# One scale total per expert, a larger VectorE share for the S4 work, and a third block of the last expert but one that multiplies by seven twice

## The chip, the cores and the metric

The program runs on one core of a Trainium2 chip. The metric is the device time of one execution in microseconds (us); the kernel before takes 2319.49 us as the median of three runs (2318.05 to 2320.9). TensorE (PE in the profile) multiplies, VectorE (DVE), ScalarE (ACT) and GpSimd (POOL) work on the elements, SyncE (SP) and GpSimd issue most of the transfers. Each engine takes its instructions strictly in the order in which the program wrote them, so an instruction that waits holds up all that stands behind it on its engine.

## The reference

2048 tokens of 512 numbers are normalized (layernorm). Two branches run on the result and are added to the input:

```python
x = A_u
xn = _layernorm(x, axis=-1)
return x + _A_ref(xn, ...) + _B_ref(xn, B_w_gate, B_w1, B_w2)
# A (S4): a kernel K[d, l] = Re(sum over n of C * exp(dt*A*l) * dt*B), 128 modes n, and a causal
#         convolution of each of the 512 channels with it by FFT, plus u * Dskip
# B (MoE): eight experts, all eight chosen for each token (K = 8), with softmax gates:
for e in range(E):
    h = _silu(xf @ w1[e]) @ w2[e]      # 512 -> 1792 -> 512
    out = out + w * h
```

## The kernel before, in words

**Experts and blocks.** The experts e run from 0 to 7, and each takes the tokens in four blocks tb of 512; (e, tb) names a block here. A float32 operand is split into a high and a low half in f16, and a product is three matmuls (high by high, high by low, low by high). The first product (x by w1) of every block but (0, 0) goes by a seven-product scheme in the manner of Strassen. The second one (hidden values by w2) is plain in the function `block`: 168 matmuls with 512 columns for a block. In `block2` it goes by seven products as well: 294 matmuls with 256 columns, while the first product falls into 588 matmuls with 128 columns where `block` has 294 with 256. The set `strong` lists the blocks that take `block2`: the four of expert 7, and (6, 1) and (6, 2).

**Weights.** One buffer holds the split weights of one expert; the next expert's are made while the last block of the one before runs and in its own first block. `piece_w1` or `piece_w1x` makes w1's (a split on ScalarE, its low part on VectorE, sums on VectorE), `piece_w2` w2's, and `piece_w2x` the four sums of w2's quarters that only `block2` uses (four sums on VectorE, a split of 1024 elements on ScalarE at L493, its low part on VectorE at L496). The place of the w2 sums (`w2x`) lies where the S4 branch has its tiles, so that `open_second` makes it only when S4 is over. `plan(e)` writes the order of these pieces out by hand, and `work_on(limit)` takes up to so many steps of them at the end of each slot.

**Slots.** A block has four quarters d with four slots s each, 16 slots in all. In `slot` the program emits some matmuls of the second product, the pieces of the next weights, and a share of S4. `bg_run` keeps an account: it gives S4 `SHARE` (0.96) times the planned TensorE time of the slot, less what VectorE was given besides, and never carries more than one slot's credit over.

**Scales.** Before its weights are split, an expert's w1 and w2 are squared on ScalarE and summed (`piece_square`, `piece_end`, `prepass_end`). Each of the two takes a total over the partitions: a matmul of one column against ones in the shared PSUM bank "s4" (`pow2_total`), a copy on ScalarE, and a few VectorE operations of one column.

**S4.** 32 chunks of 16 channels: tables on VectorE (`s4_basis` for two chunks, `s4_tables`), the kernel's matmuls (kgen, L871), the transforms of kernel and input (kf, uf), the convolution in frequency space on VectorE (`s4_conv`, L989 to L1007), the way back (yp, L1028), and `s4_out`, which scales into the tile `ysb` on ScalarE (L1036) and sends it. All of these matmuls use the bank "s4" in turn. At the first strong block, `bg_until("s4")` writes out whatever is left of S4, without any expert's matmul between, before the block starts.

Of the kernel before, what the change touches and what calls it, by code (L numbers as in the profile page):

```python
# [9 lines left out]
F32 = mybir.dt.float32  # L10
# [3 lines left out]
AF = mybir.ActivationFunctionType  # L14
# [19 lines left out]
def s4_moe_kernel(  # L34
# [151 lines left out]
    def pow2_scale(dst, st, nm, add=0):  # L186

        it = sb.tile([P, st.shape[-1]], I32, tag="p2b", name=f"it_{nm}", bufs=2)
        V.tensor_scalar(it, st.bitcast(I32), 24, 23, op0=ALU.logical_shift_right, op1=ALU.logical_shift_left)
        V.tensor_scalar(dst.bitcast(I32), it, -1.0, float((204 + add) << 23), op0=ALU.mult, op1=ALU.add)  # L190

    def pow2_inverse(dst, src, add=0):

        V.tensor_scalar(dst.bitcast(I32), src.bitcast(I32), -1.0, float((254 + add) << 23), op0=ALU.mult, op1=ALU.add)
# [258 lines left out]
        times(sc[:, 3:4], sc[:, 0:1], 1 - ASH)  # L453

    def prepass_end(e, w, n):
        r = sb.tile([P, 1], F32, tag="r2", name=f"r2_{e}_{w}")
        V.tensor_reduce(r, rows[e, w][:, :n], axis=AX.X, op=ALU.add)
        yield
        st = pow2_total(r, 1, f"w{e}_{w}")
        yield  # L460
        if bank["out"]:
            take_bank()
        if w == 0:
            sc = scales[e] = sb.tile([P, 5], F32, tag="sc", name=f"sc{e}", bufs=3)
            w1_scales(sc, st, f"w{e}")
        else:
            sc = scales[e]
            pow2_scale(sc[:, 1:2], st, f"v{e}")
            pow2_inverse(sc[:, 4:5], sc[:, 1:2])
            V.scalar_tensor_tensor(sc[:, 4:5], sc[:, 4:5], float(2.0 ** (XSH - 1 + ASH)), sc[:, 2:3], op0=ALU.mult, op1=ALU.mult)  # L470
            ge_ = sb.tile([P, NT], F32, tag="gse", name=f"gse{e}", bufs=3)
            gates_e[e] = ge_
            if e > 1:
                V.tensor_scalar(ge_, gate[:, :, e], sc[:, 4:5], None, op0=ALU.mult)

    def load_raw(e, w, pr, why):

# [14 lines left out]
    def hilo(dst, raw, sc):  # L492
        S.activation(dst[:, 0], raw, AF.Copy, scale=sc)  # L493

        def low():
            V.scalar_tensor_tensor(dst[:, 1], raw, sc, dst[:, 0], op0=ALU.mult, op1=ALU.subtract)  # L496
            clock["dve"] += tt_(raw.free_size())
        return low
# [30 lines left out]

    done = set()  # L530
    work = []
    strong = {(E - 1, tb) for tb in range(NB)} | {(E - 2, 1), (E - 2, 2)}
    live = {"n": 0, "tw": False}

    def piece_square(e, w, pr, ready):
        return Item(lambda: load_raw(e, w, pr, "pp"), [lambda raw: square(e, w, pr, raw)], ready)
# [16 lines left out]
    def piece_w2x(e, pr, ready):  # L553

        def s0(raw):
            clock["dve"] += 1.4
            it.at = now()
            for o, x, y, op in ((0, 0, 1, ALU.subtract), (1, 3, 1, ALU.subtract), (3, 0, 3, ALU.add), (2, 3, 2, ALU.subtract)):
                V.tensor_tensor(raw[:, o, :], raw[:, x, :], raw[:, y, :], op=op)

        def s1(raw):
            return hilo(second_half["w2x"][pr].rearrange("p a o d -> p a (o d)"), raw.rearrange("p o d -> p (o d)"),
                        scales[e][:, 1:2])
        it = Item(lambda: load_raw(e, 1, pr, "raw"), [s0, s1], ready)
        it.made = (e, "w2x", pr)
        return it
# [30 lines left out]
    def piece_end(e, w, n, ready):  # L597

        st = {"g": prepass_end(e, w, n)}

        def step(k):
            st["at"] = now()
            next(st["g"], None)
            done.add((e, w, k))
            clock["dve"] += (0.2, 0.0, 0.9)[k]

        def can_go():
            if "at" not in st:
                return ready()
            return now() > st["at"] + 1 and bank_free() and now() + 1 not in turns  # L610
        it = Item(None, [lambda raw, k=k: step(k) for k in range(3)], can_go)
        it.e, it.w, it.sums = e, w, False
        return [it]

    def fetch():
# [13 lines left out]
    def can(it):  # L629

        if not it.ready():
            return False
        if len(it.steps) == it.n and it.load is not None and now() < it.at + 2 and "w2 scale" in done:
            return False
        if it.sums and len(it.steps) == it.n:
            return not live["tw"]
        if it.sums and len(it.steps) == 1:
            return now() > it.at + (it.made[0] > 1)
        return len(it.steps) == it.n or it.load is None or now() > it.at
# [113 lines left out]
    def s4_basis(g):  # L753
# [61 lines left out]
        for i, o, n in ((0, 160, 128), (160, 288, 64)):  # L815
# [3 lines left out]
            V.scalar_tensor_tensor(im[:, b], zr[:, a], 2.0, im[:, a], op0=ALU.mult, op1=ALU.mult)  # L819
            V.tensor_tensor(zr[:, b], f[:, :n], r[:, :n], op=ALU.subtract)  # L820
            yield 4 * tt_(n)
        V.tensor_scalar(zi[:, 0], im, -1.0, None, op0=ALU.mult)
        s4["basis", g] = (wv, zr, zi)
        yield 0.4

    def s4_tables(c):
        g, h = c // 2, c % 2
# [204 lines left out]
        clock["pe"] += 0.68  # L1032

    def s4_out(c):
        ysb = p4.tile([P, 2, NS, DC], F32, tag="ysb", name=f"ysb{c}", bufs=1)
        S.activation(ysb, s4["yp", c].rearrange("p r d i -> p r i d"), AF.Copy, scale=s4["ks", c][:, 1:2])  # L1036
        nc.sync.dma_start(ys4[:, c * DC:(c + 1) * DC].rearrange("(m k r) d -> k r m d", k=P, r=2), ysb)

# [15 lines left out]
    def now():  # L1054
        return clock["slot"]
# [306 lines left out]
    def plan(e):  # L1362

        def at(tb):
            return lambda: (e - 1, tb) in done
        early_ = (e, 1) in strong and e == E - 2
        if (e, 0) not in strong:
            for n, w in ((0, 0), (0, 1)) + ((1, 0), (1, 1)) * early_:
                ready = at((0, 1, 2, 2)[2 * n + w] if early_ else 1 + w)
                for pr in range(NPR):  # L1370
                    work.append(piece_square(e + n, w, pr, ready))
                work.extend(piece_end(e + n, w, NPR, ready))

        def made(what, d):
            return lambda: (e - 1, NB - 1, what, d) in done and (e, "py".index(what), 2) in done
        a = [piece_w1(e, pr, made("p", d)) for d, prs in enumerate(DQS) for pr in prs]
        b = [piece_w2(e, pr, made("y", d)) for d, prs in enumerate(DQS) for pr in prs]
        free = lambda pr: (e - 1, NB - 2) not in strong or (e - 1, "w2x", pr) in done
        x = [piece_w2x(e, pr, lambda pr=pr: "pool" in second_half and (e, 1, 2) in done and free(pr)) for pr in range(NPR)]
        if (e, 0) in strong:  # L1380
            a = [piece_w1x(e, pr, made("p", d)) for d, prs in enumerate(DQS) for pr in prs]
            work.extend((x[0], x[1], a[0], x[2], a[1], x[3], a[2], a[3], b[0], b[1], a[4], b[2], a[5], a[6], b[3], x[4], b[4], x[5], b[5],
                         x[6], b[6]))
        else:
            work.extend((a[0], a[1], a[2], b[0], a[3], b[1], a[4], b[2], a[5], b[3], a[6], b[4], b[5], b[6]))
            if (e, 1) in strong:
                work.extend(x)
# [3 lines left out]
        yield from s4_all()  # L1391

    bg = background()
    SHARE = 0.96

    def bg_run():

# [162 lines left out]
    def at(n, f, where=side):  # L1560
        where.setdefault((0, n // 16, n % 16 // 4, n % 4), []).append(f)
# [80 lines left out]
    def slot(e, tb, d, s, pops):  # L1642
        for f in mid.get((e, tb, d, s), ()):
            f()
        if e + tb == 0:
            work_lows()
        if (e, tb) in strong:
            pop2(pops)
        elif order2 and order2[0] < (e, tb):
            pop2(max(9, 4 * pops))  # L1650
        elif (e, tb - 1) in strong:
            pop2(4 * pops)
        else:
            pop(pops)
        flush()
        if e == 0:
            work_lows()
        room = act_room()
        if room > 1.0 and run_later():
            room -= 1.6  # L1660
        for f in side.get((e, tb, d, s), ()):
            f()
        work_lows()
        if e + tb == 0 or tb == NB - 1:
            work_on(2 if e + tb == 0 or room > 2 and (e or d < 3) else 1)
        elif e == 0 and tb == 1:
            work_on(2 if (d, s) < (2, 1) else 1 if (d, s) == (2, 1) else 0)
        elif room > 1.0:
            work_on(1 if room < 2.2 or e else 2)
        if "pool" in second_half and work:  # L1670
            work_on(1)
        if (e, tb, d, s) >= (0, 2, 3, 1):
            if (e, tb, d, s) == (0, 2, 3, 1):
                clock["pe"] = clock["pe0"] = clock["pe1"] = clock["dve"] = clock["dve0"] = 0.0
            bg_run()
        if "s4" in done and "pool" not in second_half:
            open_second()
        clock["slot"] += 1
# [460 lines left out]
```

## Time and profile before

| | |
|---|---|
| median of three runs | 2319.49 us |
| the profiled execution | 2320.27 us, span from its first to its last instruction 2318.5 us |
| TensorE busy | 2298.7 us, 99% of the span |
| VectorE busy | 1885.1 us, 81% |
| ScalarE busy | 1520.9 us, 66% |
| GpSimd busy | 340.8 us, 15% |

The blocks follow each other without a break; (6, 0) starts at 1760.9 us and (6, 1) at 1831.9 us of the span. A block of the middle of the span takes 72 to 75 us.

### The profile page before, as it was taken

Reading aid. Unit: us, or ns where it says so; the run is one execution under the profiler, and the core shown is the slowest. Engines: PE = TensorE matmul, PEld = TensorE weight load, DVE = VectorE, ACT = ScalarE, POOL = GpSimd, SP = SyncE. Lnnn points to the kernel's source line nnn. Section 1 sums busy time; section 2 is a strip of 40 time slices with the busy share of each in tenths; the row PEclk is TensorE's granted clock in tenths of the full one; section 3 lists DMA queues with packets and bytes.
Section 4 is the critical chain, followed back from the end, with each engine's and each line's share of the span. In section 5 each row is a group of like instructions: output and inputs, shape, how many; then the busy total and the mean of one; then the engine's idle time right before and its main releaser. Section 6 shows DMA issues by size and latency. Waiting matters only on the chain.

```text
span 2318.5 us, 51756 instructions
## 1 busy us (share of the span) xinstructions
PE 2298.7 (99%) x20809; PEld 1646.6 (71%) x20809; DVE 1885.1 (81%) x3984; ACT 1520.9 (66%) x2718; POOL 340.8 (15%) x397
## 2 busy tenths in 40 slices
PE   8999999999999999999999999999999999999999
PEld 4666666666666666666666666666666689779998
DVE  8864889989999899997999989998867665775445
ACT  7676666566765666666666666676667566775655
POOL 0001001121111211011110111111111111132111
PEclk9999999999999999999999999999999999999999
DMA  8597355774666746556465654666665563586353
GB/s 277 181 264 201 98 142 125 157 153 89 150 148 144 149 87 146 141 130 142 76 150 151 128 124 93 145 176 156 134 154 133 137 135 76 130 185 120 87 109 66
DMA packets 326817, 323.82 MB, mean 140 GB/s; under 512 B 183760, under 2 KB 221008, under 8 KB 326096
## 3 DMA queue, kind: packets, MB, share of 16 engines
q1 hardware_dynamic: 270272, 226.32, 33.4%
q0 software_dynamic: 56016, 93.94, 25.8%
q8 instruction: 162, 2.65, 0.5%
q14 instruction: 79, 0.65, 0.1%
q10 hardware_dynamic: 288, 0.26, 0.0%
HBM read 209.22 MB, written 66.58 MB: 119 GB/s over the span
## 4 chain that ended last, share of the span: by engine, by line
PE 92%; DVE 4%; ACT 2%; issue 1%; DMA 1%; POOL 0%; SPq 0%; DVEq 0%; ACTq 0%; POOLq 0%
PE hb L1488 32%; PE y L1472 13%; PE y L1473 13%; PE y L1471 13%; PE hb L1839 8%; PE z L1757 7%; PE hb L2043 2%; PE kgen L871 1%; PE uf L940 1%; PE yp L1028 1%; PE kf L954 1%; DMA scB<-sE 1%; PE tp L284 0%; DVE ahl L1517 0%; DVE tm L994 0%
## 5 line engine op out<-in xcount | busy, mean ns | idle before, releaser
L1488 PE MATMUL hb<-xop,w1s 128*128 128x256 f16 x7350 | 867.2, 273 | 4.0 <-ACT scC L1992 3.9
L1488 PEld LDWEIGHTS <-w1s 128*128 128x128 f16 x7350 | 709.5, 98 | 136.1 <-issue 5.7
L1471 PE MATMUL y<-w2s,ahl 128*128 128x512 f16 x1456 | 551.9, 379 | 0.0
L1472 PE MATMUL y<-w2s,ahl 128*128 128x512 f16 x1456 | 551.8, 379 | 0.0
L1473 PE MATMUL y<-w2s,ahl 128*128 128x512 f16 x1456 | 551.8, 379 | 0.0
L1695 POOL DMA_DIRECT2D scC<-sE x124 | 111.8, 902 | 1346.4 <-ACT sE L1992 899.0
L1473 PEld LDWEIGHTS <-ahl 128*128 128x128 f16 x1456 | 142.5, 98 | 171.8
L1472 PEld LDWEIGHTS <-ahl 128*128 128x128 f16 x1456 | 142.5, 98 | 130.4
L1471 PEld LDWEIGHTS <-ahl 128*128 128x128 f16 x1456 | 142.5, 98 | 130.3
L1839 PE MATMUL hb<-xop,w1s 128*128 128x128 f16 x3528 | 212.6, 219 | 2.9 <-ACT scC L1849 2.0
L1839 PEld LDWEIGHTS <-w1s 128*128 128x128 f16 x3528 | 204.9, 98 | 8.2 <-issue 3.7
L1504 ACT ACTIVATE fa<-hb,sc 128x512 f32<-128x512 f32 (+1 forms) x204 | 129.9, 637 | 122.3 <-PE hb L1488 117.8
L1757 PEld LDWEIGHTS <-hs 128*128 128x128 f16 x1764 | 169.0, 98 | 19.3 <-DVE hs L1872 0.8
L1517 DVE SCALAR_TENSOR_TENSOR ahl<-fa,sc,ahl 128x512 f16<-128x512 f32 (+1 forms) x214 | 146.1, 683 | 29.3 <-ACT ahl L1508 29.1
L2007 ACT COPY hb<-hb 128x512 f32<-128x512 f32 x100 | 51.7, 517 | 175.2 <-PE hb L1488 174.9
L1695 POOL DMA_DIRECT2D scB<-sE x123 | 106.7, 868 | 404.6 <-ACT scB L1992 229.5
L1508 ACT ACTIVATE ahl<-fa,sc 128x512 f16<-128x512 f32 (+1 forms) x214 | 143.7, 672 | 7.6 <-DMA xnd<-xn 0.7
L859 DVE TENSOR_TENSOR table<-ta,tt 128x64 f32<-128x64 f32 (+2 forms) x192 | 132.0, 687 | 5.8
L853 DVE TENSOR_TENSOR ta<-table,zr 128x64 f32<-128x64 f32 (+2 forms) x192 | 131.7, 686 | 5.7
L995 DVE TENSOR_TENSOR s<-s,tm 128x672 f32<-128x672 f32 (+6 forms) x224 | 127.8, 570 | 7.7
L856 DVE TENSOR_TENSOR tt<-table,zi 128x64 f32<-128x64 f32 (+2 forms) x192 | 130.4, 679 | 0.0
L994 DVE TENSOR_TENSOR tm<-v,k 128x672 f32<-128x672 f32 (+6 forms) x224 | 126.6, 565 | 4.4
(332 smaller groups left out, 3299.1 us busy)
## 6 DMA issues: line engine op xcount, KB each, us to landing
xop<-xd SPq DMA_DIRECT2D x210, 256.0 KB, 3.8
pp<-in_w_dram SPq DMA_DIRECT2D x98, 512.0 KB, 4.4
raw<-in_w_dram SPq DMA_DIRECT2D x70, 512.0 KB, 4.4
oacc<-ye POOLq DMA_DIRECT2D x110, 256.0 KB, 6.3
scC<-sE POOLq DMA_DIRECT2D x87, 256.0 KB, 3.7
scB<-sE POOLq DMA_DIRECT2D x87, 256.0 KB, 3.9
raw<-in_w_dram SPq DMA_DIRECT2D x52, 256.0 KB, 3.8
raw<-in_w_dram SPq DMA_DIRECT2D x104, 128.0 KB, 4.3
```

What stands on the lines that cost most here:

```text
L853: V.tensor_tensor(ta, tin, zrv, op=ALU.mult)
L856: V.tensor_tensor(tt, tin[:, ::-1], ziv, op=ALU.mult)
L859: V.tensor_tensor(tout, ta, tt, op=ALU.add)
L1471: T.matmul(y, lhs[0], w2s[pr][:, 0, fh, :], start=(c == 0), stop=False)
L1472: T.matmul(y, lhs[0], w2s[pr][:, 1, fh, :], start=False, stop=False)
L1473: T.matmul(y, lhs[1], w2s[pr][:, 0, fh, :], start=False, stop=(c == NF - 1))
L1488: T.matmul(dst[:, q, :], w1s[pr][:, a, ORDER[e][wo], k * P:(k + 1) * P], xop[:, xo, b, k, :], start=(first_mm and q == 0 and n == 0), stop ...
L1508: S.activation(ahl[:, 0, :n], fa, AF.Copy, scale=scales[e][:, 3:4])
L1517: V.scalar_tensor_tensor(ahl[:, 1, :n], fa, sc[:, 3:4], ahl[:, 0, :n], op0=ALU.mult, op1=ALU.subtract)
L1695: nc.gpsimd.dma_start(dst, src, accum_op=ALU.add)
L1757: T.matmul(acc, t[:, a, q, :], w2_op(pr, p, b), start=(first and k == 0), stop=(c == NPR and k == 2), skip_group_check=True)
L1839: T.matmul(dst[:, q, :], w1s[pr][:, x, ORDER[e][wo], k * P:(k + 1) * P], xop[:, xo, b, k, tk], start=(first_mm and q == 0 and m == 0), sto ...
```

## The change

- `prepass_end` and `piece_end` take an expert's two totals in one matmul with two columns, after both weights have been squared. `plan` asks for one end per expert.
- (6, 0) joins `strong`. For expert 6, `plan` therefore uses `piece_w1x` and a new order, with the w2 sums late in it; `work_on` is called with a limit of 2 in the last block ahead of an expert whose first block is strong, whatever room ScalarE has.
- `can` lets no more than one first step and one second step of `piece_w2x` go in one slot.
- `SHARE` goes from 0.96 to 1.0.
- The negation at the end of `s4_basis` moves from VectorE (L822) to ScalarE, one slot later; the generator waits until it is written.
- `ysb` gets two buffers.

```diff
@@ prepass_end
+        if w == 2:
+            r = sb.tile([P, 2], F32, tag="r2", name=f"r2_{e}")
+            for k in range(2):
+                V.tensor_reduce(r[:, k:k + 1], rows[e, k][:, :n], axis=AX.X, op=ALU.add)
+            yield
+            st = pow2_total(r, 2, f"w{e}")
+            yield
+            if bank["out"]:
+                take_bank()
+            sc = scales[e] = sb.tile([P, 5], F32, tag="sc", name=f"sc{e}", bufs=3)
+            w1_scales(sc, st[:, 0:1], f"w{e}")
+            w2_scales(e, st[:, 1:2])
+            return
...
+    def w2_scales(e, st):
+        sc = scales[e]
+        pow2_scale(sc[:, 1:2], st, f"v{e}")
+        pow2_inverse(sc[:, 4:5], sc[:, 1:2])
...
-    strong = {(E - 1, tb) for tb in range(NB)} | {(E - 2, 1), (E - 2, 2)}
+    strong = {(E - 1, tb) for tb in range(NB)} | {(E - 2, 0), (E - 2, 1), (E - 2, 2)}
@@ piece_w2x
         def s0(raw):
             clock["dve"] += 1.4
-            it.at = now()
+            it.at = second_half["x0"] = now()
...
         def s1(raw):
+            second_half["x1"] = now()
@@ piece_end
-            done.add((e, w, k))
+            done.update((e, v, k) for v in ((0, 1) if w == 2 else (w,)))
@@ can
+        if it.load is not None and getattr(it, "made", (0, 0))[1] == "w2x" and second_half.get(f"x{it.n - len(it.steps)}", -1) >= now():
+            return False
@@ s4_basis
-        V.tensor_scalar(zi[:, 0], im, -1.0, None, op0=ALU.mult)
+        act_later.append((clock["slot"] + 1, lambda: S.activation(zi[:, 0], im, AF.Copy, scale=-1.0)))
         s4["basis", g] = (wv, zr, zi)
-        yield 0.4
+        while act_later:
+            yield None
@@ s4_out
-        ysb = p4.tile([P, 2, NS, DC], F32, tag="ysb", name=f"ysb{c}", bufs=1)
+        ysb = p4.tile([P, 2, NS, DC], F32, tag="ysb", name=f"ysb{c}", bufs=2)
@@ plan
-        if (e, 0) not in strong:
-            for n, w in ((0, 0), (0, 1)) + ((1, 0), (1, 1)) * early_:
-                ready = at((0, 1, 2, 2)[2 * n + w] if early_ else 1 + w)
-                for pr in range(NPR):
-                    work.append(piece_square(e + n, w, pr, ready))
-                work.extend(piece_end(e + n, w, NPR, ready))
+        if e < E - 1:
+            for n in range(1 + early_):
+                for w in range(2):
+                    ready = at((0, 1, 2, 2)[2 * n + w] if early_ else 1 + w)
+                    for pr in range(NPR):
+                        work.append(piece_square(e + n, w, pr, ready))
+                work.extend(piece_end(e + n, 2, NPR, ready))
...
         if (e, 0) in strong:
             a = [piece_w1x(e, pr, made("p", d)) for d, prs in enumerate(DQS) for pr in prs]
+            if e < E - 1:
+                work.extend((a[0], a[1], a[2], a[3], b[0], a[4], a[5], b[1], b[2], a[6], b[3], x[0], x[1], x[2], x[3], b[4], x[4],
+                             b[5], x[5], b[6], x[6]))
+                return
...
-    SHARE = 0.96
+    SHARE = 1.0
@@ slot
         if e + tb == 0 or tb == NB - 1:
-            work_on(2 if e + tb == 0 or room > 2 and (e or d < 3) else 1)
+            work_on(2 if e + tb == 0 or (e + 1, 0) in strong or room > 2 and (e or d < 3) else 1)
```

## Rows read from the trace of the kernel before

**Rows 1.** The page: busy time of each engine with its share of the span, and the shares of the engines in the chain of work that ended last.

```profile
PE 2298.7 (99%) x20809; PEld 1646.6 (71%) x20809; DVE 1885.1 (81%) x3984; ACT 1520.9 (66%) x2718; POOL 340.8 (15%) x397
...
PE 92%; DVE 4%; ACT 2%; issue 1%; DMA 1%; POOL 0%; SPq 0%; DVEq 0%; ACTq 0%; POOLq 0%
```

**Rows 2.** The stretches of single blocks, from (5, 3) to (7, 0): start and end in us, length, then busy time of PE, PEld, DVE, ACT and POOL, each with its number of instructions, the granted TensorE clock (1.00 is 2.4 GHz), the DMA engines' busy share and GB/s.

```profile
1688.60:1760.90 72.30, 72.30 (x581) 48.88 (x579) 44.79 (x89) 50.12 (x90) 9.60 (x12) 1.00 0.60 139
1760.90:1831.90 71.00, 71.00 (x513) 47.84 (x512) 56.45 (x95) 46.44 (x75) 11.31 (x13) 1.00 0.62 153
1831.90:1902.30 70.40, 67.86 (x838) 56.95 (x836) 42.43 (x77) 44.53 (x74) 10.27 (x13) 1.00 0.55 123
1902.30:1967.20 64.90, 64.90 (x885) 61.58 (x883) 32.20 (x59) 39.66 (x71) 10.51 (x14) 1.00 0.40 76
1967.20:2036.20 69.00, 65.35 (x501) 49.54 (x499) 53.47 (x90) 50.96 (x78) 9.83 (x12) 0.98 0.57 144
2036.20:2106.70 70.50, 70.11 (x848) 58.06 (x847) 44.52 (x72) 48.11 (x77) 24.30 (x29) 1.00 0.86 175
```

**Rows 3.** The waits of TensorE over the whole span: who waited for whom, us in total, times, the longest.

```profile
PE hb L1488 <- ACT scC L1992: 3.9, 3, 2.8
PE hb L1839 <- ACT scC L1849: 2.0, 3, 1.3
```

**Rows 4.** The timeline around the start of (6, 1): start, duration, engine, line, instruction, how many are merged. The first and the third row's matmuls are followed directly by the row behind them; between the last two rows two matmuls start.

```profile
1823.39 1.47 PE L1488 MATMUL hb<-xop,w1s 128*128 128x256 f16 x12
...
1824.70 0.38 PE L1471 MATMUL y<-w2s,ahl 128*128 128x512 f16 x1
...
1831.88 1.50 PE L1839 MATMUL hb<-xop,w1s 128*128 128x128 f16 x24
...
1833.22 0.38 PE L1471 MATMUL y<-w2s,ahl 128*128 128x512 f16 x1
...
1833.65 0.38 PE L1473 MATMUL y<-w2s,ahl 128*128 128x512 f16 x1
```

**Rows 5.** The timeline around the start of (6, 1): the last copy out of S4 on ScalarE and the first product's matmuls behind it, with the idle time before the instruction and what ended it in brackets.

```profile
1837.22 0.47 ACT L1036 ACTIVATE ysb<-yp,ksc 128x256 f32<-128x256 f32 x1 [6.11 <-DMA ys<-ysb]
...
1838.23 2.84 PE L1839 MATMUL hb<-xop,w1s 128*128 128x128 f16 x48 [0.97 <-ACT hb L1929]
```

**Rows 6.** The same timeline in (6, 3), and a stretch behind it with its clock (columns as in rows 2).

```profile
1996.49 1.97 ACT L493 ACTIVATE w1s<-raw,sc 128x1024 f16<-128x1024 f32 x2
...
1998.98 0.38 PE L1488 MATMUL hb<-xop,w1s 128*128 128x256 f16 x2 [2.81 <-ACT scC L1992]
...
1999.00:2010.40 11.40, 11.40 (x66) 7.23 (x66) 11.15 (x18) 8.50 (x13) 3.52 (x4) 0.85 0.65 124
```

**Rows 7.** The chain of work that ended last, in (6, 1): start, us, what.

```profile
1864.59 2.07 ACT w2x L493 x2
...
1867.08 2.17 PE hb L1839 x36
```

**Rows 8.** The instructions of single lines over the span: duration in ns (smallest, median, largest), start of the first and of the last in us, shapes.

```profile
L871 PE MATMUL kgen<-table x2048: 219/219/244, 310.1 to 1733.3; 128*32 128x64 f32 x187
...
L1036 ACT ACTIVATE ysb<-yp,ksc x32: 453/464/518, 418.4 to 1837.2; 128x256 f32<-128x256 f32 x32
...
L822 DVE TENSOR_SCALAR zi<-zi x16: 331/334/336, 260.5 to 1627.5; 128x352 f32<-128x352 f32 x16
...
L1013 ACT ACTIVATE zh<-z x32: 612/620/643, 386.6 to 1825.0; 128x512 f16<-128x512 f32 x32
...
L183 PE MATMUL tot_w<-r,ones x15: 167/167/167, 33.9 to 1723.1; 128*128 128x1 bf16 x15
```

**Rows 9.** Stretches of single blocks as in rows 2: (3, 3), (4, 0) and (4, 1), and the sum over the 17 blocks from (1, 0) to (5, 0) with the means.

```profile
1099.90:1174.30 74.40, 74.29 (x653) 50.38 (x652) 72.10 (x160) 48.52 (x86) 10.28 (x12) 1.00 0.45 93
1174.30:1247.70 73.40, 73.40 (x641) 49.64 (x640) 71.47 (x130) 48.27 (x84) 11.35 (x13) 1.00 0.61 143
1247.70:1321.30 73.60, 73.60 (x605) 50.16 (x603) 71.06 (x165) 47.72 (x94) 9.90 (x12) 1.00 0.63 140
...
sum 1248.50, PE 1248.06 PEld 845.66 DVE 1160.84 ACT 810.74 POOL 188.32; mean PE 73.42 PEld 49.74 DVE 68.28 ACT 47.69 POOL 11.08
```

**Rows 10.** Groups of VectorE's instructions by line in the 18 blocks from (1, 1) to (5, 2), 365.2 to 1688.6 us: busy us, mean ns of one, idle time before. L995 is of S4's convolution; the others are the experts' low halves.

```profile
L995 DVE TENSOR_TENSOR s<-s,tm 128x672 f32<-128x672 f32 (+6 forms) x203 | 115.8, 570 | 7.0
...
L1517 DVE SCALAR_TENSOR_TENSOR ahl<-fa,sc,ahl 128x512 f16<-128x512 f32 (+1 forms) x145 | 98.1, 677 | 9.1 <-ACT ahl L1508 9.1
L1517 DVE SCALAR_TENSOR_TENSOR ahl<-scB,sc,ahl 128x256 f16<-128x256 f32 (+1 forms) x72 | 48.9, 678 | 11.3 <-ACT ahl L1508 9.7 <-ACT st_w L178 1.6
L1517 DVE SCALAR_TENSOR_TENSOR ahl<-scC,sc,ahl 128x256 f16<-128x256 f32 (+1 forms) x72 | 48.8, 678 | 22.9 <-ACT ahl L1508 19.0 <-ACT st_w L178 3.7
L496 DVE SCALAR_TENSOR_TENSOR w1s<-tw,sc,w1s 128x1024 f16<-128x1024 f32 x28 | 35.8, 1279 | 2.5 <-ACT w1s L493 2.5
L496 DVE SCALAR_TENSOR_TENSOR w2s<-raw,sc,w2s 128x1024 f16<-128x1024 f32 x28 | 35.8, 1278 | 1.1 <-ACT w2s L493 0.7 <-ACT st_k L178 0.5
L496 DVE SCALAR_TENSOR_TENSOR w1s<-raw,sc,w1s 128x768 f16<-128x768 f32 x28 | 28.3, 1011 | 0.0
```

**Rows 11.** The timeline where an S4 matmul follows its VectorE input most closely.

```profile
1315.15 0.68 DVE L1018 SCALAR_TENSOR_TENSOR zh<-z,zh 128x512 f16<-128x512 f32 x1
...
1317.95 0.83 PE L1028 MATMUL yp<-zh,dfth 128*128 128x128 f16 x12
```

More of the change, by code (lines that the diff above doesn't have):

```diff
@@ L455, in prepass_end @@
     def prepass_end(e, w, n):
-        r = sb.tile([P, 1], F32, tag="r2", name=f"r2_{e}_{w}")
+        if w == 2:
[11 more added lines that the diff above has]
+            return
+        r = sb.tile([P, 1], F32, tag="r1", name=f"r2_{e}_{w}")
         V.tensor_reduce(r, rows[e, w][:, :n], axis=AX.X, op=ALU.add)
@@ L466, in prepass_end @@
         else:
[L467 to L474, printed above, removed]
+            w2_scales(e, st)
+    def w2_scales(e, st):
+        sc = scales[e]
+        pow2_scale(sc[:, 1:2], st, f"v{e}")
+        pow2_inverse(sc[:, 4:5], sc[:, 1:2])
+        V.scalar_tensor_tensor(sc[:, 4:5], sc[:, 4:5], float(2.0 ** (XSH - 1 + ASH)), sc[:, 2:3], op0=ALU.mult, op1=ALU.mult)
+        ge_ = sb.tile([P, NT], F32, tag="gse", name=f"gse{e}", bufs=3)
+        gates_e[e] = ge_
+        if e > 1:
+            V.tensor_scalar(ge_, gate[:, :, e], sc[:, 4:5], None, op0=ALU.mult)
     def load_raw(e, w, pr, why):
@@ L611, in piece_end @@
         it = Item(None, [lambda raw, k=k: step(k) for k in range(3)], can_go)
-        it.e, it.w, it.sums = e, w, False
+        it.e, it.w, it.sums = e, w % 2, False
         return [it]
```

## The prediction, made before the changed kernel was run

> **What bounds the kernel now.** I read the page first: TensorE is busy 99% of the span and makes up 92% of the chain that ended last; VectorE, at 81%, is next [rows 1]. So the time falls where TensorE's work falls or where it stops waiting. Then the table by block: up to (6, 0) a block's length equals TensorE's busy time, and only in (6, 1), (6, 3) and (7, 0), where strong blocks begin or end, is 2.5 + 3.7 + 0.4 = 6.6 us missing [rows 2]. The table of TensorE's waits says for whom: for ScalarE's copies that free the product's banks [rows 3]. The other engines' waits cost nothing in themselves. They matter through one question: whether S4, whose pace the account in `bg_run` sets, is over when (6, 0) begins.
>
> **The block that joins.** The trace has both kinds of matmul side by side [rows 4]: 24 with 128 columns in 1833.22 - 1831.88 = 1.34 us, 55.8 ns each; 12 with 256 in 1.31 us, 109.2 ns each; two with 512 in 0.43 us, 215 ns each. A plain block is 294 x 0.1092 + 168 x 0.215 = 32.1 + 36.1 = 68.2 us; a strong one is 588 x 0.0558 + 294 x 0.1092 = 32.8 + 32.1 = 64.9 us, which is what (6, 2) took, undisturbed [rows 2]. The edit takes 3.3 us off TensorE. That is all of its direct gain; S4's own matmuls only move to earlier blocks.
>
> A rule speaks against it. The Trainium skill, "TensorE: Matmul & The Clock Gate", section "Back-to-back issue gap", gives about 81 ns for a matmul of 128 columns in a stream of weight loads and matmuls. By it the 588 would take 47.6 us, 14.8 us more than the 32.8 of the rows, and the block would lose some 11 us. The rows above are just such a stream and show 55.8 ns; I go by them.
>
> **The last copy of S4.** At (6, 1) ScalarE waited 6.11 us for the single `ysb` to be sent, and TensorE, short of its copy, stood still for 0.97 us [rows 5]. With two buffers that wait is gone: -1.0 us.
>
> **The totals.** Seven of the fifteen for weights go. One costs TensorE a weight load and a matmul of one column, 167 ns by itself [rows 8], so between nothing and 7 x 0.167 = 1.2 us; the neighbours overlap most of it: -0.5 us. Their VectorE and ScalarE parts lie under TensorE's work, at nothing.
>
> **The negation.** On VectorE it is 16 times 0.334 us. ScalarE is not shown doing it on 352 elements; a copy of 256 takes 0.464 us and one of 512 takes 0.620 us there [rows 8], so about 0.52 us. ScalarE is at 47.7 us of 73.4 in a block [rows 9], which hides it. If that cover failed, it would delay one copy per two chunks by half a microsecond.
>
> **Does S4 end in time?** The decisive step. Kernel matmuls of 32 chunks run from 310.1 to 1733.3 us [rows 8]: (1733.3 - 310.1) / 31 = 45.9 us a chunk. The last way back was written into the start of (6, 1) at 1831.9 us; it has to come 71 us sooner, before 1760.9 us. Of VectorE's 68.3 busy us in a mean block of 73.4 [rows 9], the experts' low halves take (98.1 + 48.9 + 48.8 + 35.8 + 35.8 + 28.3) / 18 = 16.4 us [rows 10], so S4 has at most 52. The account gives it 0.04 x 73.4 = 2.9 us more a block, 5.7% more pace; over 1423 us that is 77 us. The negation's 5.3 us of VectorE are worth 5.3 x 73.4 / 52 = 7.5 us of span. So 84 us at most, for 71 needed. But not all of it comes: where S4 waits for a slot or for the bank, a larger credit is lost, and the end of the last chunk is nothing but such waits ((5, 3) has VectorE busy 44.8 us of 72.3 [rows 2]). Against that, merged totals take the bank half as often. I take four fifths, 67 us: S4 ends within a slot or so of (6, 0), and what is left when `bg_until` writes it out is the split of z (0.62 us on ScalarE, 0.68 us on VectorE [rows 8, 11]) and the way back (12 x 0.056 = 0.7 us), uncovered. A range from 0 to, with a whole convolution left, 17 us (rival 2); I take +1.0 us.
>
> **Entering and leaving strong blocks.** At (6, 1) two w2x splits of 2.07 us together held up a copy, and TensorE waited for it [rows 7]; the longest wait of that group is 1.3 us [rows 3]. The new rule in `can` forbids that pair. But the entry now lies at (6, 0), with w1's, w2's and the sums' pieces all due in (5, 3) and (6, 0) at two a slot. The trace has one entry of that kind, (6, 3) to (7, 0), and there two w1 splits (1.97 us) cost 2.81 us, after which the clock row reads 0.85 over 11.4 us [rows 6]: a stretch at the lower level, 1.2 GHz, worth 0.15 x 11.4 = 1.7 us. (7, 0) itself lost 70.50 - 70.11 = 0.4 us [rows 2]. So the new entry costs between 0.4 and 4.5 us and the old one's 1.3 goes; near the gentler of the two, since a plain (5, 3) has no pass of a strong block ending in it: 1.5 - 1.3 = +0.2 us. The old entry into expert 7 loses its pairs of w2x splits too, but gets two steps in every slot: 0, between -5 and +3 us.
>
> **VectorE's lag.** In (3, 3), (4, 0) and (4, 1) it is busy 72.10, 71.47 and 71.06 us of 74.4, 73.4 and 73.6 [rows 9]; with 2.9 more in each it would run over by 0.6, 1.0 and 0.4 us, 2 us in a row, before a block with waits gives it back. Work queued behind on VectorE is the low halves, and TensorE waits for those and for S4's. S4's nearest consumer stood 1317.95 - 1315.83 = 2.1 us behind its input [rows 11]. So a lag of 2 us just about fits: +0.3 us, between 0 and 3.
>
> **The sum**, in us: -3.3 - 1.0 - 0.5 + 1.0 + 0.2 + 0 + 0.3 = -3.3. The profiled span of 2318.5 us becomes 2315.2; that execution took 2320.27 us, 1.8 more than its span and 0.8 more than the median. On the median, 2319.5 - 3.3 = 2316.2 us, 0.14% less. About 0.2%, 4.6 us, is what can be told from no change here.
>
> **The rivals.**
> 1. The ends of the strong stretches fall quiet as well. The pairing rule then also removes the 2.81 us and the 1.7 us of lower clock behind it, and the new entry costs 0.4 instead of 1.5: 2316.2 - 4.5 - 1.1 = 2310.6 us at best, 2312.5 with a part of it. For it: every such wait in the rows has two splits on ScalarE in front [rows 6, 7]. Against it: the pair at 1996.49 us was of w1 pieces, which the rule leaves alone.
> 2. S4 isn't over, and a whole convolution stands before (6, 0). It is seven pairs of a product and a sum, 0.57 us each [rows 10], 8 us, and fourteen further operations, most of them on fewer elements, up to as much again: some 15 us on VectorE and 2 on the way back, with TensorE idle, and perhaps the lower clock behind it. 2316.2 - 1.0 + 17 = 2332 us. It decides from the point where more than about 9 us of S4 are left, since gain and threshold are 3.3 + 1.0 + 4.6. For it: the 84 us are a ceiling and the need is 71. Against it: S4 would have to come only 71 - 17 = 54 us sooner, less than two thirds of the ceiling.
> 3. The change gives back what it takes: S4 ends half a convolution late, or VectorE's lag stops TensorE in several blocks (3 us): about 2319.5 us. For it: the blocks above stand at 97% on VectorE already. Against it: TensorE is busy 1248.06 of 1248.50 us in those 17 blocks [rows 9].
> 4. Weight loads become the bound of a strong block: they are busy 61.58 of 64.90 us in (6, 2), against 48.88 of 72.30 in (5, 3) [rows 2]. If each short matmul took the mean of one load, 61.58 / 883 = 69.7 ns, instead of 55.8, the 588 of them would take 8.2 us longer: 2316.2 + 8.2 = 2324.4 us. Against it: (6, 2) is such a block, and took 64.9 us. The page named above states the same effect at a larger price.
>
> **How the numbers follow.** The forecast: 0.38, with its own range 2314.9 to 2318.5. Rival 1: 0.38, 2310 to 2314.8. Rival 2: 0.12. Rival 3: 0.11. Rival 4: 0.01. Faster by more than 0.2% comes from rival 1 and the lower edge of the forecast, 0.40; within 0.2% from the rest of it and rival 3, 0.47; slower, 0.13. The range leaves out rivals 2 and 4 and the far end of rival 1: 2310.5 to 2322.5 us. The time is that of the forecast, which ties with rival 1 but needs fewer things to go well.
>
> **What would show it.** (6, 0) about 65 us plus its entry, (6, 1) 64.9 us, no TensorE wait behind `ysb`. The last yp should lie near 1760 us, kgen should come every 43 to 44 us, and VectorE should be 71 us busy in a middle block. Wrong would be: yp well after the start of (6, 0) with TensorE idle before it, new waits for VectorE in blocks of experts 1 to 5, or a changed loss in (6, 3).

## The result: 20 us slower

The changed kernel took a median of 2339.89 us against 2320.19 us for the kernel before in the same rounds: ratio 1.0086, 95% interval 1.0073 to 1.0098. Forecast were 2316.2 us and at most 2322.5. The forecast had the wrong sign.

The page of the changed kernel: span, busy time by engine, and the chain that ended last by engine.

```profile
span 2338.5 us, 52618 instructions
...
PE 2300.7 (98%) x21222; PEld 1665.2 (71%) x21222; DVE 1904.0 (81%) x4017; ACT 1535.1 (66%) x2741; POOL 340.1 (15%) x397
...
PE 64%; DVE 21%; issue 7%; ACT 4%; DMA 2%; POOL 1%; SPq 0%; DVEq 0%; POOLq 0%; ACTq 0%
```

TensorE's busy time grew by only 2.0 us over [rows 1], while the span grew by 20: the loss is idle time. The chain says whose: VectorE's part of it went from 4% [rows 1] to 21%, though its busy share stayed at 81%.

Next, where. Of the kernel before, the stretches (1, 0) to (5, 2) and (6, 0) with (6, 1); the blocks between and behind them are in [rows 2], and so are the columns.

```profile
293.10:1688.60 1395.50, 1395.06 (x11861) 945.45 (x11860) 1288.49 (x2792) 909.79 (x1703) 210.19 (x241) 1.00 0.60 135
...
1760.80:1902.30 141.50, 138.96 (x1347) 104.88 (x1346) 98.97 (x172) 91.07 (x149) 21.58 (x26) 1.00 0.59 138
```

Of the changed kernel, (1, 0) to (5, 2), (5, 3), (6, 0) with (6, 1), and (6, 2) with (6, 3):

```profile
294.70:1711.10 1416.40, 1402.48 (x11904) 949.39 (x11903) 1305.29 (x2818) 922.21 (x1727) 209.24 (x241) 1.00 0.60 134
1711.10:1787.30 76.20, 71.94 (x512) 48.42 (x511) 59.78 (x116) 51.84 (x85) 11.14 (x13) 0.99 0.61 149
1787.30:1922.20 134.90, 133.28 (x1720) 119.32 (x1718) 85.01 (x146) 90.88 (x150) 20.65 (x25) 0.99 0.57 131
1922.20:2056.10 133.90, 128.69 (x1382) 110.28 (x1380) 85.22 (x148) 90.79 (x148) 20.30 (x24) 1.00 0.49 111
```

Length minus TensorE's busy time is its idle time. Ahead of (1, 0) the changed kernel is 1.6 us later, with 64 of S4's matmuls more and no more idle time there; (1, 0) to (5, 2) cost +20.9 us, of which 13.92 - 0.44 = 13.5 are idle; (5, 3), 1688.6 to 1760.8 us before, +4.0; the joined blocks give -6.6; behind them nothing changes (0.1). Sum: 20.0 us. So (6, 0) and (6, 1) together get shorter by more than was hoped (how much of that is due to the joining, a run below tells), and everything is lost **before** them, in blocks whose TensorE work the change hardly touches.

What TensorE waited for in (1, 0) to (5, 2) of the changed kernel: us in total, times, longest. The kernel before has one such wait there, of 0.3 us.

```profile
PE hb L1513 <- ACT hb L2022: 4.2, 3, 2.4
PE hb L1513 <- DMA xop<-xd: 2.2, 1, 2.2
PE tot_k L183 <- DVE krow L910: 1.9, 1, 1.9
PE hb L1513 <- DVE w1s L512: 1.6, 1, 1.6
PE hb L1513 <- ACT scC L2017: 1.4, 3, 1.0
PE kf L974 <- DVE kh L936: 1.4, 1, 1.4
```

No one releaser stands out. A dozen short waits, for copies on ScalarE, for a reload of `xop`, for S4's own pieces on VectorE, are what it looks like when one engine runs late and several in-order queues hand its lateness on.

### The profile page after: what moved, and what is told of

It is laid out like the page before. It is cut to its first block, busy times and chain, and to the rows that moved or that the text cites. A ratio compares the mean times of both kernels' runs of the same rounds, so it can differ in the third digit from the quotient of the medians.

```text
span 2338.5 us, 52618 instructions
## 1 busy us (share of the span) xinstructions
PE 2300.7 (98%) x21222; PEld 1665.2 (71%) x21222; DVE 1904.0 (81%) x4017; ACT 1535.1 (66%) x2741; POOL 340.1 (15%) x397
## 4 chain that ended last, share of the span: by engine, by line
PE 64%; DVE 21%; issue 7%; ACT 4%; DMA 2%; POOL 1%; SPq 0%; DVEq 0%; POOLq 0%; ACTq 0%
PE hb L1513 20%; PE hb L1864 10%; PE z L1782 9%; PE y L1496 7%; PE y L1497 7%; PE y L1498 7%; DVE ahl L1542 3%; DVE w1s L512 2%; DVE tm L1014 2%; DVE s L1015 2%; DVE tt L876 2%; DVE table L879 2%; DVE ta L873 1%; DVE w2s L512 1%; PE kgen L891 1%
## 5 line engine op out<-in xcount | busy, mean ns | idle before, releaser
L1513 PE MATMUL hb<-xop,w1s 128*128 128x256 f16 x7056 | 833.9, 273 | 16.7 <-ACT scC L2017 6.3
L1496 PE MATMUL y<-w2s,ahl 128*128 128x512 f16 x1400 | 530.6, 379 | 0.2 <-ACT ye L1471 0.2
L1498 PE MATMUL y<-w2s,ahl 128*128 128x512 f16 x1400 | 530.6, 379 | 0.0
L1497 PE MATMUL y<-w2s,ahl 128*128 128x512 f16 x1400 | 530.6, 379 | 0.0
L1498 PEld LDWEIGHTS <-ahl 128*128 128x128 f16 x1400 | 137.0, 98 | 165.2 <-issue 0.2
L1864 PE MATMUL hb<-xop,w1s 128*128 128x128 f16 x4116 | 248.9, 219 | 2.0 <-ACT scC L1874 2.0
L1497 PEld LDWEIGHTS <-ahl 128*128 128x128 f16 x1400 | 137.0, 98 | 125.8 <-issue 0.4
L1496 PEld LDWEIGHTS <-ahl 128*128 128x128 f16 x1400 | 137.0, 98 | 125.3
L1782 PEld LDWEIGHTS <-hs 128*128 128x128 f16 x2058 | 197.0, 98 | 22.3 <-DVE hs L1897 0.9
L1529 ACT ACTIVATE fa<-hb,sc 128x512 f32<-128x512 f32 (+1 forms) x196 | 124.8, 637 | 113.3 <-PE hb L1513 109.8
L1542 DVE SCALAR_TENSOR_TENSOR ahl<-fa,sc,ahl 128x512 f16<-128x512 f32 (+1 forms) x206 | 140.8, 684 | 39.9 <-ACT ahl L1533 39.6
L876 DVE TENSOR_TENSOR tt<-table,zi 128x64 f32<-128x64 f32 (+2 forms) x192 | 130.6, 680 | 20.9 <-ACT zi L841 20.9
L1782 PE MATMUL z<-w2x,hs 128*128 128x256 f16 x1176 | 144.8, 273 | 0.4 <-DVE hs L1897 0.4
L1533 ACT ACTIVATE ahl<-fa,sc 128x512 f16<-128x512 f32 (+1 forms) x206 | 138.3, 672 | 8.0 <-DMA xnd<-xn 1.3
```

What stands on the lines that cost most here:

```text
L876: V.tensor_tensor(tt, tin[:, ::-1], ziv, op=ALU.mult)
L1496: T.matmul(y, lhs[0], w2s[pr][:, 0, fh, :], start=(c == 0), stop=False)
L1497: T.matmul(y, lhs[0], w2s[pr][:, 1, fh, :], start=False, stop=False)
L1498: T.matmul(y, lhs[1], w2s[pr][:, 0, fh, :], start=False, stop=(c == NF - 1))
L1513: T.matmul(dst[:, q, :], w1s[pr][:, a, ORDER[e][wo], k * P:(k + 1) * P], xop[:, xo, b, k, :], start=(first_mm and q == 0 and n == 0), stop ...
L1542: V.scalar_tensor_tensor(ahl[:, 1, :n], fa, sc[:, 3:4], ahl[:, 0, :n], op0=ALU.mult, op1=ALU.subtract)
```

## The experiments

Three theories from the start. **V**: with SHARE 1.0, VectorE is given more than it does in the time, lags, and stops TensorE through whatever stands behind it. **W**: the negation on ScalarE, for which VectorE now waits, does it. **J**: the joined block or its weight work loses by itself. All of the following start from the changed kernel; ratios are against the kernel before in the same rounds.

**The negation back on VectorE.**

```diff
-        act_later.append((clock["slot"] + 1, lambda: S.activation(zi[:, 0], im, AF.Copy, scale=-1.0)))
+        V.tensor_scalar(zi[:, 0], im, -1.0, None, op0=ALU.mult)
...
-        while act_later:
-            yield None
+        yield 0.4
```

> The changed kernel with one edit undone: the negation in s4_basis stands on VectorE again (L822 of before). S4 is written out at the same pace and ends at the same place. Theory V (SHARE = 1.0 fills VectorE over its slots, the lag stops TensorE): the 20.9 us that VectorE waited for the negation were mostly taken out of idle time, so the time stays within 5 us of the changed kernel, 2335 to 2341 us, and TensorE's stops in (2,1), (4,1) stay. Rival W (the new wait of VectorE for ScalarE's negation makes the lag): nearly all of the loss comes back, 2318 to 2325 us, and the stops in (2,1), (4,1) are gone.

Measured: 2334.63 us, ratio 1.0065 (1.0048 to 1.0082). That is just under V's band and far above W's. The start of (5, 3) came at 1702.9 us instead of 1711.1, and (2, 1) still has a stop of 2.1 us. So at SHARE 1.0 W explains 5 us of the 20. What that move cost stands in the table of VectorE's waits of the changed kernel, (1, 0) to (5, 2):

```profile
DVE ahl L1542 <- ACT ahl L1533: 40.0, 16, 6.9
DVE tt L876 <- ACT zi L841: 20.6, 7, 4.6
```

It saved VectorE 16 x 0.334 = 5.3 us of work [rows 8] and had it stand idle for 20.6 us, as the negation waits its turn in ScalarE's queue behind copies that wait for TensorE.

**SHARE back at 0.96**, the negation left on ScalarE; and **both back**.

```diff
-    SHARE = 1.0
+    SHARE = 0.96
```

> The changed kernel with SHARE at 0.96 again, the negation still on ScalarE. S4 then ends later: bg_until writes out the end of the last chunk, from its last sums on, ahead of (6,0). Theory V: the stops in blocks of experts 1 to 5 (about 14 us of waits, 4 us of low clock) go to under 3 us, the end of S4 costs 3 to 8 us at (6,0): 2322 to 2330 us. Rival W: the waits for the negation stay, and with them the stops: 2335 us or more, with the end of S4 on top.

> Both undone: negation on VectorE and SHARE 0.96; the merged totals, the third strong block, its order and the second ysb buffer stay. Theory V and rival W both expect the stops of experts 1 to 5 gone; what is left is the joining block (about -6 us over (6,0) and (6,1), as in the changed kernel) and the end of S4 at (6,0), 3 to 8 us: 2316 to 2323 us. If it is at 2335 us, the loss lies in the other edits (totals, two steps a slot).

Measured: 2339.03 us, ratio 1.0084 (1.0069 to 1.0099), and 2340.64 us, ratio 1.0089 (1.0074 to 1.0104). Neither is faster than the changed kernel. Both lie outside V's bands; the first lies in W's, and the second where it was to be put down to the other edits. The stretches of the first of the two (columns and order as above) tell V and W apart:

```profile
293.10:1692.00 1398.90, 1396.76 (x11931) 946.52 (x11929) 1298.06 (x2802) 920.82 (x1727) 210.17 (x241) 1.00 0.60 136
1692.00:1785.50 93.50, 74.35 (x557) 50.62 (x550) 72.02 (x142) 54.08 (x91) 10.43 (x12) 0.90 0.56 138
1785.50:1920.70 135.20, 133.59 (x1718) 119.63 (x1717) 84.95 (x146) 90.55 (x150) 20.58 (x24) 0.99 0.54 119
```

The first row has lost its idle time (2.1 us are left) and is 17.5 us shorter: V holds for experts 1 to 5. The second row has all of it back, 93.5 us for (5, 3), and the waits of that stretch name one place:

```profile
PE yp L1048 <- ACT ysb L1056: 17.2, 1, 17.2
PE yp L1048 <- DVE zh L1038: 1.5, 1, 1.5
```

At 1784.1 us TensorE had stood still for 17.2 us until the last convolution of S4 was through VectorE: the prediction's rival 2, in its place and at its price of 17 us. The 3 to 8 us that both expectations gave to the end of S4 were too few. With the negation on VectorE as well (5, 3) took 93.5 us too, so at 0.96 the negation's place makes no difference that can be told. The share moves the loss from one place to the other, and (6, 0) begins at nearly the same time, 1785.5 us against 1787.3.

**(6, 0) a plain block again**, all else as changed.

```diff
-    strong = {(E - 1, tb) for tb in range(NB)} | {(E - 2, 0), (E - 2, 1), (E - 2, 2)}
+    strong = {(E - 1, tb) for tb in range(NB)} | {(E - 2, 1), (E - 2, 2)}
```

> The changed kernel without its strong block (6,0): that block is plain as in before, S4 is over before it. All else as changed (SHARE 1.0, negation on ScalarE, merged totals). Theory V and rival W: the stops of experts 1 to 5 stay, the gain of the block goes: 2340 to 2345 us. Rival J (the loss comes from joining (6,0): two steps a slot in (5,3), S4's end): most of the loss goes, 2318 to 2325 us.

Measured: 2336.27 us, ratio 1.0069 (1.0054 to 1.0084). That is between the two bands. The stops in experts 1 to 5 stayed, start of (5, 3) at 1708.9 us, so J does not explain them: 16 us of loss are there without the joined block. But the block did not pay either, for without it the time is 3.6 us shorter. The stretches (5, 3) and (6, 0) with (6, 1):

```profile
1708.90:1780.40 71.50, 71.20 (x513) 47.86 (x512) 50.86 (x99) 46.66 (x80) 10.64 (x13) 1.00 0.59 143
1780.40:1917.50 137.10, 136.15 (x1299) 102.09 (x1297) 71.31 (x113) 87.90 (x142) 21.05 (x26) 1.00 0.57 136
```

Of the 6.6 us that (6, 0) with (6, 1) lost in the changed kernel, 4.4 go here with a plain (6, 0): S4 is over before it, and so are most of the waits at the entry. The joining itself brought 137.1 - 134.9 = 2.2 us there and cost 76.2 - 71.5 = 4.7 us in (5, 3).

**That, with SHARE 0.96 and the negation on VectorE.** Of the change the merged totals, the second `ysb`, the rule in `can` and the two steps a slot in (6, 3) are left.

> The changed kernel with SHARE back at 0.96, the negation back on VectorE, and (6,0) a plain block: S4 then ends in its own pace before (6,1), as in the kernel before, so nothing is written out uncovered. What is left of the change is the merged totals and the second ysb buffer. Theory V (the lag of a VectorE filled to 1.0 and, at 0.96, the uncovered last convolution are together the whole loss): both are gone, and 1.0 + 0.5 us of small gains stand: 2316 to 2321. Theory J (the joined block or the merged totals lose by themselves): the totals are still merged, so 2325 or more.

Measured over eleven runs: 2320.8 us, ratio 1.0006 (0.9997 to 1.0015). The whole loss is gone, as V has it. Three edits are undone at once here, so it takes the runs above to say which does what. Against the 2340.64 us with both back it differs in the joined block alone: at 0.96 the joining costs 20 us, because S4's end then stands uncovered in front of (6, 0). Nothing of the 1.5 us foreseen for the two small parts is seen in the total; the interval allows a gain of 0.7 us at most. The stretches (1, 0) to (5, 2) and (6, 0) with (6, 1) show more:

```profile
293.80:1693.50 1399.70, 1397.45 (x11932) 946.85 (x11930) 1296.67 (x2815) 914.46 (x1710) 210.03 (x241) 1.00 0.60 135
1765.30:1903.20 137.90, 137.38 (x1322) 103.49 (x1321) 84.60 (x139) 88.10 (x143) 21.53 (x26) 1.00 0.56 133
```

The idle time at the entry fell from 141.50 - 138.96 = 2.5 to 0.5 us, with `ysb`'s 1.0 and the pair of w2x splits in it. What was won there, (1, 0) to (5, 2) gave back: 4.2 us longer, 1.8 of it idle, the rest TensorE's work, with 71 more matmuls, S4's that come sooner.

**SHARE 0.99 and 0.98**, the negation on VectorE, (6, 0) strong.

> The changed kernel with SHARE 0.99 and the negation on VectorE; (6,0) is strong, and by the order written out S4 still ends as early as in the changed kernel, so no long uncovered convolution. A dose between 0.96 (no stops in experts 1 to 5) and 1.0 (2334.6 us with the negation on VectorE). Theory V: the lag grows with the share, so the start of (5,3) lies between 1692 and 1703 us and the time at 2326 to 2333. If instead the lag sets in with a step at 1.0 (whole slots), 2316 to 2322; if the share does nothing, as with 1.0, 2334 to 2335.

> The changed kernel with SHARE 0.98 and the negation on VectorE, between 0.96 (start of (5,3) at 1692.4 us, then a wait of 17.2 us for S4's last convolution) and 0.99 (1703.8 us, with 4 us of that wait left). By the order written out S4 ends here as at 0.96, some five slots later than at 0.99. If the lag is a dose of the share: start of (5,3) between 1694 and 1702 us, and the whole 2342 to 2350, the worst of both. If the lag sets in only with the place at which S4's chunks fall in the slots: start of (5,3) within 2 us of 1692.4 us and the whole 2338 to 2342.

Measured: 2335.79 us, ratio 1.0071 (1.0056 to 1.0085), and 2338.04 us, ratio 1.0075 (1.0060 to 1.0090). The start of (5, 3) for 0.96, 0.98, 0.99 and 1.0 is 1692.4, 1700.9, 1703.8 and 1702.9 us; the idle time before it, 2.2, 6.5, 9.6 and 10.6 us. So the lag is a dose up to 0.99, though half of it comes with the first two hundredths. Each total fell outside the band that went with that reading: 0.99 cost as much as 1.0, and 0.98 less than the 2342 us foreseen, in the band of the other reading. In front of (6, 0) S4's last way back stopped TensorE for 4.7 us, and a copy behind a piece of w1, whose sums stood on VectorE behind S4's convolution, for 4.5 us, not for 17. I had taken its place in the order for the same as at 0.96; the trace has 24 matmuls of the last two ways back in (5, 3) against 36, so it was not.

**VectorE relieved, at SHARE 1.0.** One line of the convolution is left out, and nothing else changes, the plan included.

```diff
                 V.tensor_tensor(tm, v3f[:, :, 0:n], kb, op=ALU.mult)
-                V.tensor_tensor(s3[:, :, m:], s3[:, :, m:], tm, op=ALU.add)
```

> The changed kernel, SHARE 1.0 and the negation on ScalarE, order of the work unchanged, but the seven additions that gather the short products of each of S4's convolutions (some 4 us of VectorE per chunk of 45 us) are left out, so that the convolution keeps only its first term. Nothing else differs, and VectorE now has less to do than it was given. Theory V: VectorE keeps up, the stops of experts 1 to 5 go, the start of (5,3) is at 1694 us or sooner, and the time is 2314 to 2323, what the change would have brought with VectorE's costs right. If the stops come from the place of the work in the slots, or from the negation's wait, and not from VectorE's lag: 2332 to 2340.

Measured over ten runs: 2322.19 us, ratio 1.0012 (1.0002 to 1.0021). This is the test that V could have failed: same share, same order, same negation on ScalarE, and 17.7 us of the 20 are back, and the time lies in V's band. The start of (5, 3) missed its mark of 1694 by 2 us. The stretches:

```profile
295.10:1696.20 1401.10, 1397.55 (x11905) 947.82 (x11904) 1190.30 (x2609) 921.73 (x1727) 209.47 (x241) 1.00 0.60 135
1696.20:1770.90 74.70, 71.38 (x513) 47.88 (x512) 52.22 (x101) 51.71 (x85) 11.11 (x13) 1.00 0.61 153
1770.90:1905.00 134.10, 132.48 (x1720) 118.54 (x1718) 84.97 (x146) 90.93 (x150) 20.69 (x25) 1.00 0.58 131
```

It took 1305.29 - 1190.30 = 115 us of VectorE in the first stretch to get there, and 3.5 us of idle time stayed in it, 3.3 in (5, 3). So even with VectorE relieved the change was not faster than the kernel before. One thing this run does not separate: the line left out also makes each chunk's own chain shorter by some 4 us, so that S4's matmuls find their inputs sooner.

VectorE waited for the negation here as well, and so it did at SHARE 0.96. In (1, 0) to (5, 2) of the relieved kernel:

```profile
DVE tt L876 <- ACT zi L841: 36.9, 11, 8.1
```

With SHARE 0.96 and the negation on ScalarE:

```profile
DVE tt L876 <- ACT zi L841: 19.1, 7, 5.3
```

TensorE was idle for 3.5 and 2.1 us in these stretches. In these runs W's wait cost something only where VectorE had no room besides.

**Who hands the lateness on?** In (2, 1) of the changed kernel TensorE stopped for 2.2 us at 672.5 us for a reload of `xop`. SP's queue in front of it (start, duration, queue, line, transfer):

```profile
664.20 0.42 SPq L916 DMA_DIRECT2D kd<-ksb  x1
667.88 1.76 SPq L918 DMA_DIRECT2D kt<-kd  x4
669.74 0.85 SPq L2013 DMA_DIRECT2D xop<-xd  x2
```

The loads of `kt` came 3.3 us after `kd` was issued, which they wait for to land, and the reload stood behind them. Two ways of parting them:

```diff
-                nc.sync.dma_start(xop[:, xo], xd[nxt][:, xo])
+                nc.scalar.dma_start(xop[:, xo], xd[nxt][:, xo])
```

> The changed kernel with the reloads of xop (in the plain and the strong blocks) issued from ScalarE's queue instead of SP's. In the changed kernel one stop of 2.2 us, at 672.5 us, waits for such a reload whose issue stood in SP's queue behind a load of kt that waited for S4's late kernel row. If SP's queue is a main carrier of the lag: 2 to 6 us faster than the changed kernel (2334 to 2338). If the lag reaches TensorE mainly through ScalarE's copies and the banks: within 1.5 us of it, or slower, since an issue on ScalarE stands in front of the hb copies.

```diff
-            nc.sync.dma_start(kt[32 * jh:32 * jh + 32], kd[:, jh, :].rearrange("(s x) c -> x s c", s=4))
+            nc.gpsimd.dma_start(kt[32 * jh:32 * jh + 32], kd[:, jh, :].rearrange("(s x) c -> x s c", s=4))
```

> The changed kernel with the four loads of kt of each chunk issued from GpSimd's queue instead of SP's, so that the reloads of xop behind them no longer stand behind a wait for kd's landing. In the changed kernel TensorE stops for 2.2 us at 672.5 us for an xop reload that SP issued only at 669.7 us, after kt's at 667.9 us, and a stretch at half clock follows. If SP's queue passes S4's lateness on to TensorE there: the stop goes, (2,1) falls from 81.6 us to 78 us or less, and the time is 2334 to 2338. If that wait is only where the lateness happens to show, and it shows elsewhere without it: (2,1) or its neighbours stay as long together, 2338 to 2341. Slower than 2341 only if GpSimd's issues delay the sums of scB and scC.

Measured: 2350.35 us for the first, ratio 1.0133 (1.0118 to 1.0147): a wait on ScalarE's queue stands in front of the copies that free the banks, and those waits grew from 1.4 to 12.3 us in experts 1 to 5. The second: 2339.39 us, ratio 1.0091 (1.0074 to 1.0107), the changed kernel's time. The wait for `xop` is gone from its table of waits; 650 to 900 us:

```profile
PE yp L1048 <- ACT k L978: 3.7, 1, 3.7
PE kgen L891 <- ACT ysb L1056: 1.8, 1, 1.8
PE kf L974 <- DVE kh L936: 1.4, 1, 1.4
```

1.8 us of it come back in the same block and 3.7 us two blocks later. In these two runs a queue is where the lateness shows, not where it is from; with one queue mended it showed at the next.

## Why the prediction was wrong, step by step

**The joined block** was right for TensorE's work. (6, 0) and (6, 1) fell from 141.5 to 134.9 us. TensorE's busy time in them fell by 138.96 - 133.28 = 5.7 us; S4's 48 matmuls that left, at 0.056 us each, are 2.7 of that, and the other 3.0 are the block, against 3.3 in the sum. (6, 1), now without its entry, took 65.6 us. By an estimate from the Trainium skill's 81 ns for a matmul of 128 columns ("TensorE: Matmul & The Clock Gate", section "Back-to-back issue gap") it would have taken 14.8 us more, so here too the trace disagrees with that figure. What the sum missed is the price in (5, 3): all told the joining cost 3.6 us at SHARE 1.0.

**Entering** cost 1.6 us of idle time in (6, 0), 1.5 in the sum. (6, 2) with (6, 3) did not change by 0.1 us: rival 1 stayed away. `ysb`'s 1.0 us is seen at the entry of the kernel with a plain (6, 0) and not in its total; **the totals**, -0.5 us, cannot be told from noise.

**"VectorE's lag" is the step that failed**: +0.3 us, at most 3. By the stretches it was the 20.9 us of (1, 0) to (5, 2) less what S4's earlier matmuls account for (43 more matmuls, 2.4 us), so about +18.5, the negation's 5 among them: 13.5 us of idle time and 5 us more of TensorE's busy time. I had the lag itself: three blocks, 2 us run over, S4's nearest consumer 2.1 us behind its input [rows 9, 11]. I then let a reserve of 2.1 us meet a lag of 2 and called it covered. As I read it now, a block that happens to have room does not reset the lag, since the account then gives that room to S4 as well; that was the point of SHARE 1.0. No run tests this by itself. And I looked only at direct consumers, not at who stands behind a late one on ScalarE and SP. Rival 3 had the right mechanism and 3 us for it.

What I did not look at is the account's own prices. It books an operation on n elements at n / 960 + 0.1 us (`tt_`), so 0.9 + 2 x 3.5 = 7.9 us for the fifteen products and sums of one convolution. In S4's last convolution with SHARE 0.96 and the negation on ScalarE VectorE did nothing else between these two starts:

```profile
1772.10 0.96 DVE L1009 TENSOR_TENSOR s<-v,k 128x768 f32<-128x768 f32 x1
...
1781.42 0.43 DVE L1024 TENSOR_TENSOR zq<-s 128x256 f32<-128x256 f32 x1
```

They took 9.3 us, 1.4 more than booked, or 3% of a chunk of 45 us. A share of 0.96 leaves room for that, one of 1.0 does not. This fits V; no run changed the prices.

**The negation** at nothing was wrong by 5 us. Its duration was foreseen well (0.52 us; it took 0.479 to 0.549). The price was the other way round: what the moved instruction *waits behind* on its new engine, and VectorE idle for it.

**"Does S4 end in time?"** was right in its answer by luck, and its working was wrong. S4's last way back came just ahead of (6, 0), and 4.3 us of idle time in (5, 3) stand against +1.0 in the sum, within its range. But it came only 1831.8 - 1787.2 = 44.6 us sooner, where 67 were foreseen; it was in time because the blocks were late too. The 84 us of ceiling supposed that a larger credit becomes a quicker S4. Chunks came every (1683.5 - 288.4) / 31 = 45.0 us, against 45.9 before and 43 to 44 foreseen, and in time, not in slots, the settings hardly differ: in the six kernels with (6, 0) strong that differ in the share and the negation alone, (6, 0) began at 1779.9 to 1787.3 us, where 1763.5 us was wanted (1760.8 and the 2.7 us of S4's matmuls that come sooner). What the credit bought was paid for in TensorE's waits.

The sum I should have made is VectorE's up to (6, 0). In the changed kernel that is 1305.3 + 59.8 = 1365.1 us from (1, 0) on, against 1333.2 before: 14.0 us left the joined blocks (98.97 to 85.01), and more came in that I had not counted. Part of it are the pieces of w1: at two steps a slot six of the seven fall into (5, 3), where three did. Their groups on VectorE there:

```profile
L598 DVE TENSOR_TENSOR raw<-raw 128x256 f32<-128x256 f32 x24 | 10.1, 424 | 0.8
L512 DVE SCALAR_TENSOR_TENSOR w1s<-raw,sc,w1s 128x1024 f16<-128x1024 f32 x6 | 7.6, 1279 | 2.0 <-ACT w1s L509 2.0
L512 DVE SCALAR_TENSOR_TENSOR w1s<-raw,sc,w1s 128x768 f16<-128x768 f32 x6 | 6.0, 1013 | 0.6 <-ACT w1s L509 0.6
```

That is 23.7 us, where the kernel before had 13.1 in the same block for half as many low halves and the sums of `piece_w1` (3.8 + 3.1 + 2.8 + 1.7 + 1.7). For no loss, the 1305.3 us of (1, 0) to (5, 2) would have had to fit into 1395.5 + 2.4 us, 93.4% busy over 19 blocks, with S4's tail, mostly waits, still to come in (5, 3). The highest of these kernels held 1298.06 / 1398.90 = 92.8% there, and had the wait of 17 us behind it. That makes the plan a tight one; that it had to fail is argued from it, not shown.

What stays open: why 0.99 costs as much as 1.0, and 0.98 nearly so, while 0.96 costs next to nothing in (1, 0) to (5, 2). And of the relieved kernel's remaining 2.6 us only the places are known, 3.1 us more idle time in (1, 0) to (5, 2) and 3.3 in (5, 3), not the reason. No version that beats the kernel before was found.

## What to carry to other kernels

When background work has to end earlier, add up its engine's work to the new deadline and divide by the time; a share in a planner makes no time, and here VectorE's lateness came out as waits of TensorE. The busy share alone does not show where that begins: VectorE was busy 92.3% of (1, 0) to (5, 2) in the kernel before, with 0.4 us of TensorE idle, and 92.2% in the changed kernel, with 13.9. A share a little below 1 may be the margin for costs that run higher than planned: before it goes, look at who stands behind that engine in every in-order queue. And an instruction that is moved to an idle engine is priced by what it stands behind there and by who now waits for it, not by its own duration.

## What was not expected of the hardware

A stop of 2.2 us took more than itself. The stretches behind the one at 672.5 us of the changed kernel:

```profile
672.00:674.00 2.00, 1.48 (x9) 1.10 (x10) 1.83 (x11) 0.00 (x0) 0.00 (x0) 0.70 1.03 299
674.00:676.00 2.00, 2.00 (x11) 1.45 (x10) 1.97 (x10) 0.00 (x0) 0.00 (x0) 0.50 0.89 263
676.00:678.00 2.00, 2.00 (x14) 1.27 (x13) 1.93 (x5) 0.99 (x2) 0.00 (x0) 0.95 1.02 381
```

The granted clock fell to 0.50, the lower level of 1.2 GHz, while TensorE was already busy again. With 0.70, 0.50 and 0.95 over 2 us each, up to 0.6 + 1.0 + 0.1 = 1.7 us were lost on top, an estimate from these rows. In (1, 0) to (5, 2) the changed kernel has 7.4 us more of TensorE's busy time, and the 43 additional matmuls are 2.4 us of it; the other 5 us fit such stretches, though I did not trace each.
